# Half of one projection and a quarter of another by Strassen blocks in the prologue of a two-branch attention kernel

## The chip, the cores and the metric

The kernel runs on one core of one Trainium2 chip. The metric is the device time of one execution in microseconds; the runs of a kernel are given by their median. The engines are named as the profile names them: PE (matmuls; PEld is its weight load), DVE, ACT, POOL and SP, whose queue issues most DMAs.

## What is computed

x has 2048 tokens of 1024 features. A linear-attention branch A and a softmax-attention branch B share x, have 32 heads of 32 features each, and are mixed by a gate per token:

```python
g = _sigmoid((x * gate_w).sum(-1, keepdims=True))
# A: phi(t) = where(t > 0, t + 1, exp(t)) + 1e-6
kv  = einsum("bhsd,bhse->bhde", phi(k), v)
z   = einsum("bhsd->bhd", phi(k))
num = einsum("bhqd,bhde->bhqe", phi(q), kv)
den = einsum("bhqd,bhd->bhq", phi(q), z)[..., None] + 1e-6
a   = (num / den) @ A_wo
# B
p = softmax(einsum("bhqd,bhkd->bhqk", q, k) * Dh ** -0.5)
b = einsum("bhqk,bhkd->bhqd", p, v) @ B_wo
return g * a + (1 - g) * b
```

Each branch has its own wqkv (1024 x 3072), so the projections x @ wqkv are most of the dense work.

## The kernel before

**Numbers in two parts.** Every projection operand is split into a high part (rounded to fp32r) and a low part; a product is three matmuls, high x high, high x low, low x high (`three`, L146 to L158). A split is one ACT cast (L302) and one subtraction, on DVE (L297, by `split`) or on POOL (L869, by `split_w`). A full matmul is 128 x 128 weights by 512 columns.

**Prologue.** J counts two halves of the tokens. For each, `v_pass` computes B's v for its first 512 of 1024 columns directly, over eight row pieces k, into all eight PSUM banks, and `v_out` (L369) copies them out and stores them. Beside it DVE forms the sums of x that Strassen's method needs (`sides`, `split_sides`, `last_side`). Then eight quads compute B's q and k by Strassen's method: seven products in place of eight, with `quad_weights` preparing the next quad's weight sums and splits, and `quad` combining the products on DVE and storing q and k. A generator `wo_parts` runs beside the quads on POOL and prepares sums of wo. The weights of v are kept in a ring of tile halves (`RINGW`, `ring_w`), stored (`store_wv`, q `wv<-big`) and reloaded for J = 1. In the last quad, `leave` splits the weights of the first linear chunk on DVE and `load_first` loads q and k of heads 0 and 1 by POOL's DMA queue (L1224, L1237).

**The linear stream.** After the prologue everything is a stream of units, one per chunk of 512 output columns and tile of 128 tokens, 24 matmuls each. The chunks in order: v's second half (1 chunk, 16 units), four kv chunks (256 key and 256 value columns, 64 units), two q chunks, two o chunks. A kv unit applies phi (ACT L918 to L920, DVE L1147), adds the keys for z on POOL (L1150, L1152) and multiplies keys by values in small matmuls (`keys`, L938). Weights of the next chunk are loaded and split while the last unit of a chunk runs: on DVE if the chunk that ends is v, else on POOL (`renew`, `split_w`).

**The heads.** Softmax attention of the 32 heads of B runs in the same time as the units. `maxima` computes the scores of a head once for their maxima (PE L1263, DVE L1268). `heads_` computes them again, transposed, with the maximum subtracted, and ACT takes the exponent (PE L1405, ACT L1408) into one of nine tiles `pr_t`. POOL sums the tiles for the denominator (L1486 the first, L1490 the others; 1536 of 2048 columns, DVE takes the other 512 in L1506; beside q units POOL takes all). Every eight tiles, PE multiplies them by v (L1555). At a head's end POOL issues two accumulating DMAs that fold the sum (L1444, L1445); `finish` multiplies it by ones on PE (L1327), at the next head's first L1555 group, and DVE divides. `rows` transposes the maxima once per head (L1280).

**The planner.** The order of instructions on every engine is written out at build time. The loop at the end keeps a planned clock T for each engine, with costs as constants (0.2275 us a matmul, 0.15 + 0.0022 us per column for a POOL sum), and picks the stream that can start. Linear units are paced against score steps: `rates` is the number of matmul slots per step (64 steps of L1405 per head), computed from `cost`, the slots of all kv, q and o units. Before the heads begin there is a warm-up: `warm` slots of linear units and the maxima of head 0 and the first 12 of head 1, which are spread over it (`behind`). SP's and POOL's queues are in order like the engines.

**The gate.** `gate_step` takes one of 32 pieces of x every GATE_STEP planned microseconds: SP loads it, ACT scales it by the gate weights (L594), POOL adds it up (L600), and PE sums over partitions (L608). Before, this lies in the warm-up, beside v's second half.

Of the kernel before, what the change touches and what calls it, by code (L numbers as in the profile page):

```python
# [19 lines left out]
P = 128  # L20
DH = 32
# [17 lines left out]
WARM = 8  # L39
NE = 3  # L40
AHEAD_X = 3
PIECE_STEP, PIECE_REST = 3.4, 2
GATE_STEP, GATE_FROM = 2.3, 20.0
# [6 lines left out]
def kernel(  # L50
# [271 lines left out]
    for side in PLACES:  # L322
        side["X12"] = side["T4"]
    NQB = 8
    RINGW = [(16, 0), (16, 1), (17, 0), (17, 1), (19, 0), (19, 1), (14, 0), (14, 1), (20, 0), (20, 1), (15, 0),
             (18, 0), (18, 1)]
# [4 lines left out]
    def ring_w(n, p):  # L331

        b, half = RINGW[n % len(RINGW)]
        return big[b][:, (2 * half + p) * C:(2 * half + p + 1) * C]

    def v_ring(J, k):
        return J * (NK + QUADS * NP) + k

    def quad_ring(J, f, s):
        return v_ring(J, NK) + f * NP + s  # L340
# [14 lines left out]
    assert not {b for b, _ in RINGW[:NK]} & set(RAW_BIG)  # L355
# [7 lines left out]
    v_outs = [[P1, C11, H11, *halves(zrep), W2, *halves(zrep)], [P1, C11, W2, H11] * 2]  # L363
    wv_d = [dram.tile([P, 2 * C], F32, name=f"wv{k}") for k in range(NK)]
# [147 lines left out]

    def wo_piece(m, i):
        half, l = int(m[1]) - 1, int(m[2]) - 1
        return b_wo[(2 * i + l) * P:(2 * i + l + 1) * P, half * C:(half + 1) * C]
# [58 lines left out]
    gate_x = [mid[7], mid[8], mid[9], zrep[:, :C]]  # L574

    def gate_step():
# [11 lines left out]
        raw, acc = gate_x[n % len(gate_x)], (mid[6], zrep[:, C:])[j % 2]  # L588
# [45 lines left out]
    def split_wv(raw, k):  # L634
        split(ring_w(k, 0), ring_w(k, 1), raw, nc.vector)
# [35 lines left out]
    def late_side(J):  # L671

        yield
        yield
        last_side(J, (0, 1))
        yield
        last_side(J, (2, 3))

# [5 lines left out]
    def quads(J, first, *others):  # L684

        sides_ = [late_side(J), *others]
        for f in range(QUADS - 1):
# [4 lines left out]
            quad(J, f, beside(quad_weights(raws_q[(f + 1) % 2], J, f + 1), *sides_))  # L692
# [9 lines left out]
    for k in range(NK):  # L702
# [12 lines left out]
        if k == 4:  # L715
            load_quad(raw_a, 0)
        if k >= 5:
            store_wv(((0, 1, 2), (3, 4, 5), (6, 7))[k - 5])
        if k == 6:
            for _ in spill(0, "X12"):  # L720
                pass
    for b in RAW_BIG:
        big[b] = big_tile(b, F32R)
    w_t[2] = big[18]
    quad_w = quad_weights(raw_a, 0, 0)
    for _ in range(3):
        next(quad_w)
    split_sides(raw_x0[3], 0, 3)
    for _ in quad_w:
        pass  # L730
    load_quad(raw_b, 1)
    for t, to in enumerate(v_outs[0]):
        v_out(0, t, bank[t], to)

# [21 lines left out]
    quad(0, QUADS - 1, change())  # L756
    for k in range(NK):
# [5 lines left out]
        elif k == 1:  # L763
            sides(raw_x1[1], 1)
            split_sides(raw_x1[1], 1, 1)
            load_pair(raw_x1[3], 1, 3)
        elif k == 2:
            for kk in (4, 5):
# [3 lines left out]
        elif k == 3:  # L772
# [5 lines left out]
            load_quad(raw_a, 0)  # L778
            for _ in spill(1, "X12"):
                pass  # L780
        elif k == 4:
            split_sides(raw_x1[3], 1, 3)
            load_quad(raw_b, 1)
        elif k == 5:
            quad_w = quad_weights(raw_a, 1, 0)
            next(quad_w)
            next(quad_w)
        elif k == 6:
            for _ in quad_w:
                pass  # L790
# [3 lines left out]
    def load_v1(raws, ks):  # L794
        for raw, k in zip(raws, ks):
            dma(raw, b_wqkv[k * P:(k + 1) * P, 2 * D + C:2 * D + 2 * C])

    def split_v1(raw, k):
        split(wpart(k, 0), wpart(k, 1), raw, nc.vector)

    quads(1, lambda: load_v1(raw_a, range(KH)), spill_rest(1), parts)
    load_v1(raw_b, range(KH, NK))

    def leave():

        split_v1(raw_a[2], 2)
        split_v1(raw_a[3], 3)
        yield
        split_v1(raw_a[0], 0)
        split_v1(raw_a[1], 1)  # L810
        yield
        for k in range(KH, NK):
            split_v1(raw_b[k - KH], k)
# [18 lines left out]
    chunks = [("v", c) for c in range(1, NQC)] + [("kv", c) for c in range(D // HC)]  # L832
# [21 lines left out]
    def load_w(kind, c, k, n):  # L854
        if kind == "v":
            raw = load_cols(b_wqkv, vcols(c), k, n)
        elif kind == "kv":
# [42 lines left out]
    def token(i, t):  # L900
        return (t + NT // 2) % NT if chunks[i][0] == "v" else t
# [162 lines left out]
    def linear():  # L1064
        extra = iter(())
        for n, (i, t) in enumerate(units):
            kind, c = chunks[i]
            follow = chunks[i + 1] if i + 1 < len(chunks) else None
            lag = 2 if kind == "v" else 0
# [879 lines left out]
```

## Time and profile before

| what | value |
|---|---|
| median of 3 runs (lowest, highest) | 2807.05 us (2806.37, 2807.08) |
| span of the profiled execution | 2803.6 us, 3.4 us under the median |
| PE busy, PE weight load busy | 2794.3 us, 2040.4 us |
| DVE busy | 2327.5 us |
| ACT busy | 1640.2 us |
| POOL busy | 2104.4 us |
| granted clock | 1.000 |

A row of a group names line, engine, operation, tile written <- tiles read, shape and count; then busy time and mean nanoseconds of one; then the engine's idle time before these instructions and what ended it. Busy digits are tenths of each of 40 slices. Window rows give the length, then busy microseconds (and instructions) of PE, PEld, DVE, ACT and POOL, the clock, the DMA share and GB/s. The profiled execution is one execution; its span runs from the first to the last instruction, and the timed runs contain a little more around it.

### The profile page before, as it was taken

Reading aid. Unit: us, or ns where it says so; the run is one execution under the profiler, and the core shown is the slowest. Engines: PE = TensorE matmul, PEld = TensorE weight load, DVE = VectorE, ACT = ScalarE, POOL = GpSimd, SP = SyncE. Lnnn points to the kernel's source line nnn. Section 1 sums busy time; section 2 is a strip of 40 time slices with the busy share of each in tenths; the row PEclk is TensorE's granted clock in tenths of the full one; section 3 lists DMA queues with packets and bytes.
Section 4 is the critical chain, followed back from the end, with each engine's and each line's share of the span. In section 5 each row is a group of like instructions: output and inputs, shape, how many; then the busy total and the mean of one; then the engine's idle time right before and its main releaser. Section 6 shows DMA issues by size and latency. Waiting matters only on the chain.

```text
span 2803.6 us, 46986 instructions
## 1 busy us (share of the span) xinstructions
PE 2794.3 (100%) x15880; PEld 2040.4 (73%) x15880; DVE 2327.5 (83%) x3745; ACT 1640.2 (59%) x3095; POOL 2104.4 (75%) x1150
## 2 busy tenths in 40 slices
PE   9999999999999999999999999999999999999999
PEld 8888888776677767777667777776676667666687
DVE  7978956888888888888888888888887888886688
ACT  5334323666676666666666676676666666666522
POOL 0642543799999999999899988889889988888000
PEclk9999999999999999999999999999999999999999
DMA  8997979433444334333433444455575555544774
GB/s 286 314 327 232 319 225 287 153 99 107 104 120 109 99 95 125 99 102 97 135 98 102 107 129 133 148 175 178 176 222 145 147 159 150 144 122 150 253 234 152
DMA packets 403340, 459.52 MB, mean 164 GB/s; under 512 B 106894, under 2 KB 234894, under 8 KB 401308
## 3 DMA queue, kind: packets, MB, share of 16 engines
q1 hardware_dynamic: 381084, 419.03, 48.6%
q0 software_dynamic: 22016, 37.50, 6.3%
q8 instruction: 126, 2.06, 0.3%
q14 instruction: 114, 0.93, 0.1%
HBM read 314.31 MB, written 127.66 MB: 158 GB/s over the span
## 4 chain that ended last, share of the span: by engine, by line
PE 91%; DMA 3%; DVE 1%; issue 1%; SPq 0%; ACT 0%; ACTq 0%; DVEq 0%
PE bank L1405 17%; PE bank L1263 17%; PE bank L1555 16%; PE bank L153 13%; PE bank L158 13%; PE bank L156 13%; PE bank L1327 1%; PE bank L1049 1%; DMA big<-wv 1%; SPq L170 0%; DMA big<-ra 0%; DMA xs<-big 0%; PE bank L938 0%; DMA mid<-in_xT 0%; DMA extra<-in_xT 0%
## 5 line engine op out<-in xcount | busy, mean ns | idle before, releaser
L1490 POOL TENSOR_TENSOR big<-big,big 128x512 f32<-128x512 f32 (+2 forms) x694 | 1642.0, 2370 | 106.9 <-ACT big L1408 63.8
L1268 DVE TENSOR_REDUCE mx<-bank 128x1 f32<-128x512 f32 x2048 | 1314.3, 684 | 301.1 <-PE bank L1263 297.5
L1408 ACT ACTIVATE big<-bank 128x512 f32<-128x512 f32 x2048 | 1180.0, 602 | 427.8 <-PE bank L1405 362.4
L1405 PE MATMUL bank<-big,big 128*128 128x512 f32 x1888 | 741.5, 394 | 0.1
L1263 PE MATMUL bank<-big,big 128*128 128x512 f32 x1888 | 739.0, 391 | 0.0
L153 PE MATMUL bank<-big,big 128*128 128x512 f32 x1576 | 616.0, 391 | 2.8 <-ACT big L302 1.2
L156 PE MATMUL bank<-big,big 128*128 128x512 f32 x1576 | 614.2, 390 | 0.0
L158 PE MATMUL bank<-big,big 128*128 128x512 f32 x1572 | 613.2, 390 | 0.2 <-DMA big<-xs 0.2
L1555 PE MATMUL bank<-big,mid 128*32 128x512 f32 x4096 | 454.2, 593 | 0.0
L1405 PEld LDWEIGHTS bank<-big,big 128*128 128x128 f32 x1888 | 354.0, 188 | 124.7 <-issue 47.4
L1263 PEld LDWEIGHTS bank<-big,big 128*128 128x128 f32 x1888 | 354.5, 188 | 73.7 <-ACT big L1408 1.4
L153 PEld LDWEIGHTS bank<-big,big 128*128 128x128 f32 x1576 | 296.0, 188 | 69.5 <-ACT big L302 2.6
L158 PEld LDWEIGHTS bank<-big,big 128*128 128x128 f32 x1572 | 295.1, 188 | 63.6 <-DVE big L297 1.0
L156 PEld LDWEIGHTS bank<-big,big 128*128 128x128 f32 x1576 | 295.9, 188 | 61.3 <-DVE big L297 0.2
L1555 PEld LDWEIGHTS bank<-big,mid 128*32 128x32 f32 x4096 | 143.6, 110 | 264.3 <-issue 264.0
L1506 DVE TENSOR_TENSOR bank<-bank,big 128x512 f32<-128x512 f32 x364 | 252.2, 693 | 5.5 <-ACT big L1408 3.3
L302 ACT CAST big<-mid 128x512 fp32r<-128x512 f32 (+1 forms) x157 | 92.9, 618 | 122.5 <-DVE mid L1674 66.0
L1486 POOL TENSOR_TENSOR big<-big,big 128x1536 f32<-128x1536 f32 (+1 forms) x31 | 123.4, 3980 | 40.3 <-ACT big L1408 40.1
L153 PE MATMUL bank<-big,xh 128*128 128x512 f32 x376 | 147.0, 391 | 0.6 <-DVE mx L1268 0.6
L158 PE MATMUL bank<-big,xh 128*128 128x512 f32 x376 | 146.9, 391 | 0.3 <-DMA xh<-xs 0.3
L156 PE MATMUL bank<-big,xh 128*128 128x512 f32 x376 | 146.8, 390 | 0.0
L1563 ACT COPY mid<-bank 128x512 f32<-128x512 f32 x32 | 18.8, 587 | 212.8 <-PE bank L1555 205.8
(165 smaller groups left out, 2226.4 us busy)
## 6 DMA issues: line engine op xcount, KB each, us to landing
big<-xs SPq DMA_DIRECT2D x288, 256.0 KB
big<-qk SPq DMA_DIRECT2D x690, 64.0 KB
xh<-xs SPq DMA_DIRECT2D x144, 256.0 KB
qk<-mid SPq DMA_DIRECT2D x128, 256.0 KB
big<-oA SPq DMA_DIRECT2D x84, 256.0 KB
xs<-big SPq DMA_DIRECT2D x64, 256.0 KB
oA<-mid SPq DMA_DIRECT2D x64, 256.0 KB
big<-big POOLq DMA_DIRECT2D x50, 256.0 KB, 5.4
```

The lines of the kernel that those rows point to most:

```text
L153: yield nc.tensor.matmul(ps, sh, mh_, start=(kt == 0), stop=False)
L156: yield nc.tensor.matmul(ps, sh, ml_, start=False, stop=(late and last))
L158: yield nc.tensor.matmul(ps, sl, mh_, start=False, stop=last)
L302: nc.scalar.copy(hi, src)
L1263: nc.tensor.matmul(bank[b], q[:, t % TPC * P:(t % TPC + 1) * P], k[:, j * C:(j + 1) * C], start=True, stop=True)
L1268: nc.vector.tensor_reduce(m[:, t, j:j + 1], bank[b], AX.X, ALU.max)
L1405: nc.tensor.matmul(bank[b], k[:, t * P:(t + 1) * P], q_cols(h, j), start=True, stop=True)
L1408: nc.scalar.activation(pr_t[i][:, j * C:(j + 1) * C], bank[b], AF.Exp, scale=SCALE)
L1486: nc.gpsimd.tensor_add(lacc[:, :qp], pr(0)[:, :qp], pr(1)[:, :qp])
L1490: nc.gpsimd.tensor_add(lacc[:, sl], lacc[:, sl], pr(t)[:, sl])
L1506: nc.vector.tensor_add(lacc[:, qp:] if t == NT - 1 else l_b[:, :n], l_b[:, :n], src)
L1555: nc.tensor.matmul(av_b[j * DH:(j + 1) * DH, :], v[:, t, :], pr(t)[:, j * C:(j + 1) * C], start=(t == 0), stop=(t == NT - 1))
```

## The change

v's second half and the first of the four kv chunks leave the linear stream. After each `v_pass`, a new function `block` computes both for that half of the tokens as one 2 x 2 Strassen product: weight column half 1 is v's second half, column half 2 the 256 key and 256 value columns. The seven products run in the order below. Products that belong to the same output accumulate in PSUM without being copied out first (`onto`). Weights are loaded by `load_side`, summed on DVE (`sums`) and POOL (`sums4`) and split on DVE, one product ahead, between two alternating sets of ring places (`SETS`). Keys and values of the chunk go through phi, the z sums (POOL) and the small key products inside the block, and a partial z per J goes through DRAM (`zs_d`).

The first quad's weights, which were prepared at the end of `v_pass`, are now prepared in the block's last products. The linear stream starts with the second kv chunk, whose weights `leave` splits on DVE. The warm-up is seven units long instead of sixteen. The gate's pieces come every 4.5 planned us instead of 2.3, so that they reach into the first heads, and use three loading tiles instead of four.

```diff
+WARM_UNITS = 7
-GATE_STEP, GATE_FROM = 2.3, 20.0
+GATE_STEP, GATE_FROM = 4.5, 20.0
...
+    BLOCK = [("X11", "W11"), ("X21", "W12"), ("T2", "S2"), ("T1", "S1"), ("T3", "S3"), ("T4", "W22"), ("X22", "S4")]
...
+    def block(J, w11, w12, w21, w22, quad_w, renew):
...
+        steps = {
+            (0, 0): lambda: split_n(1, w12, 0, 1),
+            (0, 1): lambda: split_n(1, w12, 2, 3),
+            (0, 2): lambda: sums(0),
+            (0, 3): lambda: sums(1),
+            (1, 0): lambda: (sums(2), split_n(2, w11, 0, 1)),
...
+            (1, 2): lambda: (split_n(2, w11, 3), sums4(), load_quad(raw_a, 0), last_side(J, (0,))),
...
+            (5, 3): lambda: (early_kv(2, 3), renew(), next(quad_w), z_sums(range(4))),
+            (6, 0): lambda: (later_kv(0, 1), next(quad_w)),
...
+        for n, (name, m) in enumerate(BLOCK):
+            onto = name in ("T2", "T3", "T4", "X22")
+            at = 0 if name in ("X11", "T2", "T3", "T4") else TPC
+            for kt in range(KH):
+                wh, wl = (ring_w(SETS[J][n % 2][kt], p) for p in range(2))
+                for i in range(TPC):
+                    xh_, xl_ = (xpiece(J, name, p, kt)[:, i * P:(i + 1) * P] for p in range(2))
+                    for u, (x_, w_) in enumerate(((xh_, wh), (xh_, wl), (xl_, wh))):
+                        nc.tensor.matmul(bank[at + i], x_, w_, start=(kt == u == 0 and not onto),
+                                         stop=(kt == KH - 1 and u == 2), skip_group_check=onto)
...
+        if k == 3:
+            load_side(raw_a, "W11")
+        elif k == 4:
+            load_side(raw_big[0], "W21")
         if k >= 5:
             store_wv(((0, 1, 2), (3, 4, 5), (6, 7))[k - 5])
         if k == 6:
+            load_side(raw_big[1], "W12")
+            for i in range(2):
+                block_split(0, 0, i, raw_a[i])
             for _ in spill(0, "X12"):
                 pass
-    quad_w = quad_weights(raw_a, 0, 0)
...
+        elif k == 7:
+            load_side(raw_big[2], "W22")
...
     for t, to in enumerate(v_outs[0]):
         v_out(0, t, bank[t], to)
+    split_sides(raw_x0[3], 0, 3)
...
+    block(0, raw_a, raw_big[1], raw_big[0], raw_big[2], quad_weights(raw_a, 0, 0), renew_0)
...
-    chunks = [("v", c) for c in range(1, NQC)] + [("kv", c) for c in range(D // HC)]
+    chunks = [("kv", c) for c in range(1, D // HC)]
...
-                next_w.append((follow, k, mark, nc.vector if kind == "v" else nc.gpsimd))
+                next_w.append((follow, k, mark, nc.gpsimd))
...
-    warm = (NQC - 1) * NT * pace
-    cost = {"kv": NT * (D // HC) * (pace + 1) + 2 * (D // HC), "q": NQC * NT * (pace + 2),
+    warm = WARM_UNITS * pace
+    cost = {"kv": NT * (D // HC - 1) * (pace + 1) + 2 * (D // HC) - warm, "q": NQC * NT * (pace + 2),
             "o": NQC * NT * pace}
...
-            part = (lin_done[0] - 6 * pace) / (warm - 7 * pace) if warm else 1.0
+            part = (lin_done[0] - pace) / (warm - 2 * pace)
```

`pace` is 24, the slots of a unit; `lin_done` counts the slots done. `block` for J = 1 is called in the same way after the second `v_pass`.

241 lines of the change are left out of this document (169 added, 72 removed).

## The prediction

> **What bounds the kernel now.** I read the page first, its busy times and slices:
>
> ```profile
> span 2803.6 us, 46986 instructions
> PE 2794.3 (100%) x15880; PEld 2040.4 (73%) x15880; DVE 2327.5 (83%) x3745; ACT 1640.2 (59%) x3095; POOL 2104.4 (75%) x1150
> POOL 0642543799999999999899988889889988888000
> PEclk9999999999999999999999999999999999999999
> ```
>
> PE has no idle time to speak of and its clock never drops. A busy PE could still be a slow one, so the timeline of PE comes second, in the last projection product before the linear stream:
>
> ```profile
> 398.73 0.39 PE L153 MATMUL bank<-big,big 128*128 128x512 f32 x1
> ...
> 400.09 0.39 PE L153 MATMUL bank<-big,big 128*128 128x512 f32 x1
> ```
>
> Six matmuls start in 1.36 us, one every 0.2267 us. That is the price of a full matmul here; work taken off PE is worth its price as long as nothing else is as late as PE. The POOL digits ask whether that holds: 0 to 7 tenths in the prologue (the first seven slices), 8 and 9 in the heads. So the third view is the heads, in which three things share PE: the maxima of one head, the probabilities of another, and the linear units that fill in. One row transpose (L1280) is issued per head; the first row below has 18 of them, all in heads that run beside kv units. The next two count the matmuls of line 153, one in three of a linear unit's, in the same stretch.
>
> ```profile
> L1280 PE MATMUL bank<-ident,mneg x18: 270/271/272, 557.9 to 1644.2; 128*16 128x128 f32 x18
> L153 PE MATMUL bank<-big,big 128*128 128x512 f32 x312 | 122.0, 391 | 0.0
> L153 PE MATMUL bank<-big,xh 128*128 128x512 f32 x160 | 62.6, 391 | 0.0
> ```
>
> 17 heads take 1086.3 us, so PE needs 63.9 us a head, and (312 + 160) x 3 / 17 = 83.3 of its matmuls belong to linear units.
>
> What does POOL need for a head? It sums the probabilities (L1486, L1490), issues two DMAs that fold the sum (L1444, L1445), and adds the keys for z (L1152). A stretch where POOL is behind and never waits gives its own pace: from the fold of one head at 1420.6 us to the fold three heads later at 1600.0 us.
>
> ```profile
> 1420.60:1480.20 59.60, 59.60 (x404) 41.96 (x403) 51.25 (x89) 38.15 (x75) 57.97 (x30) 1.00 0.36 95
> 1480.20:1540.00 59.80, 59.80 (x388) 41.29 (x387) 51.31 (x88) 38.70 (x77) 57.81 (x29) 1.00 0.40 107
> 1540.00:1600.00 60.00, 60.00 (x405) 42.26 (x404) 51.53 (x89) 39.00 (x75) 58.44 (x30) 1.00 0.38 99
> L1490 POOL TENSOR_TENSOR big<-big,big 128x1536 f32<-128x1536 f32 x30 | 106.2, 3538 | 1.8
> L1490 POOL TENSOR_TENSOR big<-big,big 128x512 f32<-128x512 f32 x36 | 46.0, 1285 | 2.1
> L1486 POOL TENSOR_TENSOR big<-big,big 128x1536 f32<-128x1536 f32 x3 | 12.9, 4293 | 0.0
> L1152 POOL TENSOR_TENSOR mid<-mid,mid 128x256 f32<-128x256 f32 x10 | 8.9, 893 | 0.0
> L1445 POOL DMA_DIRECT2D big<-big x3 | 4.3, 1418 | 0.0
> L1444 POOL DMA_DIRECT2D big<-big x4 | 4.0, 1008 | 1.6 <-POOL big L1490 1.6
> ```
>
> (The windows' columns after the length are PE, PEld, DVE, ACT and POOL.) The groups show 174 us of work and only short hand-over gaps, no wait for another engine. So POOL's own head is 59.8 us, with 3.3 z-adds in it. Once per 16 units, that is every 4.6 heads, eight weight subtractions (L869) of 1.3 us come on top, 2.2 us a head:
>
> ```profile
> L869 POOL TENSOR_TENSOR big<-big,big 128x512 fp32r<-128x512 f32 x27 | 34.7, 1298 | 8.4 <-ACT big L867 6.6 <-PE bank L156 1.5 <-DMA mid<-in_a_wqkv 0.3
> ```
>
> PE is the bound by 63.9 to 62.0: a lead of three per cent, and it exists only because linear units sit in the heads. The change takes units out of exactly there.
>
> How much lateness can POOL afford? What waits for it first is the fold: PE's matmuls on the folded sum (L1327) stand at a fixed place in PE's order, in the next head's first product of probabilities and values.
>
> ```profile
> L1486 POOL TENSOR_TENSOR big<-big,big x31: 3496/4133/4628, 518.1 to 2531.7; 128x1536 f32<-128x1536 f32 x26, 128x2048 f32<-128x2048 f32 x5
> 577.36 1.46 POOL L1445 DMA_DIRECT2D big<-big  x1
> DMA to landing us min/median/max: 6.2/6.2/6.2
> 598.56 0.62 PE L1327 MATMUL bank<-big,ones 64*32 64x256 f32 x9
> ...
> 1420.62 1.42 POOL L1445 DMA_DIRECT2D big<-big  x1
> DMA to landing us min/median/max: 6.8/6.8/6.8
> 1429.21 0.45 PE L1327 MATMUL bank<-big,ones 64*32 64x256 f32 x8
> ```
>
> For the first head the fold lands at 583.6, 15.0 us before PE asks. For the head in which a set of weights was split, it lands at 1427.4, only 1.8 us before. One split set ate the slack; the next heads give it back at 63.9 - 59.8 = 4 us each.
>
> **The change part by part.** *PE work.* v's second half was 16 units of 24 matmuls, and the first kv chunk 16 more: 768. By Strassen it is two blocks of 7 products x 4 row pieces x 4 tiles x 3 = 336: 672. 96 matmuls less, x 0.2267 = -21.8 us. The small key products of those 16 units become two batches with as many matmuls:
>
> ```profile
> L938 PE MATMUL bank<-mid,mid 128*32 128x32 f32 x1024 | 15.7, 199 | 0.0
> ```
>
> 15.7 us for 64 units is 0.25 a unit, 4 us for 16; batching can save at most a part of that, and I take 0. Nothing hides the 21.8 us but what is late next.
>
> *Length of a head.* The planner's rate for kv and o units is (kv cost + o cost - 24) over 1728 steps. Before: (1608 + 768 - 24)/1728 = 1.361 matmul slots a step, 87.1 a head. After, the kv cost is 48 units x 25 + 8 - 7 x 24 = 1040, so (1040 + 768 - 24)/1728 = 1.032, 66.1 a head, 63.2 of them matmuls of units (24 of 25). PE's head becomes 63.9 - 20.1 x 0.2267 - 0.2 (0.84 units at 0.25) = 59.1 us. POOL's becomes 59.8 - 0.7 z-adds x 0.89 = 59.2 us. They are equal: from here on, whatever else POOL has to do in the kv heads (1040/66.1 = 15.7 of them) stands in full on the path once the slack is gone.
>
> *Gate.* Its POOL adds now end before the heads begin:
>
> ```profile
> L600 POOL TENSOR_TENSOR mid<-mid,mid x10: 1272/1290/1295, 428.5 to 483.4; 128x512 f32<-128x512 f32 x10
> L600 POOL TENSOR_TENSOR zrep<-zrep x4: 1286/1290/1463, 457.6 to 507.6; 128x512 f32<-128x512 f32 x4
> L1405 PE MATMUL bank<-big,big x1888: 387/389/504, 508.5 to 2633.0; 128*128 128x512 f32 x189
> ```
>
> They cost nothing there, since POOL was idle. After, the heads begin after 168 unit slots and 76 maxima, 244 x 0.2267 = 55 us, some 60 with the key products; the first sum follows 10 us later (508.5 to 518.1). The gate steps every 4.5 us from 20 us on, its add 8 us behind: by 70 us nine of 32 steps are through, and about 20 of the 28 adds remain, x 1.29 = 25.8 us on POOL in heads 0 and 1. Its 32 loads on SP and 32 scalings on ACT (ACT is at 39 of 60 us above) fit; one accumulating DMA that POOL issues for z is 1.4 us, as L1445, and lies within the ends below. Of POOL's lateness, the first head has 15.0 us of slack, less what PE's shorter head takes: the 80.5 us from the first sum to L1327 become 80.5 x 59.1/63.9 = 74.5. So 25.8 - 15.0 + 6.0 = 16.8 us of waits by the end of head 1.
>
> *Splits.* Before, four sets come in kv heads; after, the first is split by DVE in the prologue, and those for the third and fourth kv chunk and for q remain. Two lie amid kv heads: 2 x 8 x 1.3 = 20.8 us, with no slack left. The q set falls where q units lengthen the heads; 3 us for it. The other 14 heads at 0.1: 1.4 us. POOL in all: 16.8 + 20.8 + 3 + 1.4 = 42. Ends: if PE's head proves 1 us longer than reckoned, or POOL's shorter, 14 us are given back, and if some gate adds come earlier another 6: 22. The other way: 55.
>
> These are waits of 6 to 11 us on PE, and the trace has none like them:
>
> ```profile
> 560.00:1640.00 1080.00, 1079.87 (x6981) 760.67 (x6980) 938.03 (x1588) 718.27 (x1391) 1013.32 (x507) 1.00 0.39 106
> ```
>
> In this stretch of heads PE is idle for 0.13 us and the granted clock is 1.00, so I price a wait at its length. [...]
>
> *Entering the first block.* ACT copies eight banks out before it can cast the weights of the second product; the seventh copy waits for a tile still being stored.
>
> ```profile
> 47.63 1.64 SPq L170 DMA_DIRECT2D v<-mid  x3
> 49.38 1.92 SPq L170 DMA_DIRECT2D v<-zrep  x2
> 53.88 1.22 ACT L369 COPY zrep<-bank 128x512 f32<-128x512 f32 x2 [3.85 <-DMA v<-zrep]
> 24.00:44.00 20.00, 20.00 (x90) 16.57 (x89) 19.73 (x32) 9.85 (x19) 0.00 (x0) 1.00 1.09 362
> ```
>
> Before, the first quad's weights were cast ahead of these copies. After, SP has W21, W12 and W22 queued ahead of the stores in place of one quad load: 2 MB more, at the 362 GB/s of the last row 6 us. The copy comes at 60, then another, four casts and a subtraction (0.5 to 0.6 each: 9.85 us for ACT's 19, 19.73 for DVE's 32 in that row): 63. The first product (48 matmuls, 10.9 us) starts when the pass ends, where the stores begin, 47.8, and ends at 58.7. So 4 us; between 0, if DMAs overlap better, and 9. In the second block the loads are far ahead: 0. Inside the blocks DVE and ACT have per product (10.9 us) four splits and four adds, some 5 us each at these prices: hidden.
>
> *Earlier maxima.* The planner lets the maxima begin after 24 unit slots instead of 144: the first comes about 6 us into the stream instead of 33; the keys for its second quarter come by POOL's queue:
>
> ```profile
> 402.93 2.46 POOL L1237 DMA_DIRECT2D big<-qk  x5
> DMA to landing us min/median/max: 5.0/5.6/5.9
> L1263 PE MATMUL bank<-big,big x1888: 387/389/583, 432.2 to 2572.4; 128*128 128x512 f32 x189
> ```
>
> The stream began near 399.4; the fifth maximum would come at about 407 and its keys land at about 409, those of the third quarter a few us later: 3 us (0 to 6). Behind this wait stand only units, on the same PE.
>
> Sum: -21.8 + 42 + 4 + 3 = +27, with the ends -21.8 + 22 = 0 and -21.8 + 55 + 9 + 6 = +48. Against the profiled span of 2803.6 that is 2831; the median of the runs, 2807.05, lies 3.4 us above the span for what is around it, and I carry this over: 2834. I place the forecast a little lower, at 2830, since the slack of 15 us is the tightest of POOL's deadlines and not all of them.
>
> **Rivals.** (1) *POOL keeps up, and the matmuls saved are seen.* If PE's head stays over POOL's by 2 us or more (units pulled later, more key products, fold landing earlier than asked), 15 heads return 30 us, which with the initial slack covers gate and splits. For it: before, four split sets cost PE nothing. Against it: that took 4 us a head, and 20.1 matmuls are gone. It decides at a POOL head of about 57.5 us. Time: 2807 - 21.8 + 4 + 0 to 4 = 2791, or 2785 to 2797 with the ends of the small terms. (2) *The two cancel.* POOL costs 15 to 25 us: 2802 to 2812. [...] (4) *DVE becomes the bound.* In the 1080 us of heads above it is busy for 938, 55.5 of 63.9 us a head: that is 94% of 59.1. It would add under 5 us to any case.
>
> **How the numbers follow.** Forecast 0.53 (2813 to 2845), rival 1 0.27, rival 2 0.13 (half of it on either side of 2807), rival 3 0.07. About 0.2%, 5.6 us, is what a measurement of this kernel can tell from no change. Faster by more: 0.27; within: 0.13; slower: 0.53 + 0.07 = 0.60. The range of 2788 to 2846 leaves out a third of rival 1, most of rival 3 and little else.
>
> **What would show it.** Right: in the kv heads the fold lands when L1327 asks, PE's L1327 or its weight load shows idle time put down to POOL or the fold's DMA, POOL is over 97% busy from the first head to the q units, and the L1280 period is about 60 to 62 us, longer in heads 0 and 1. The block's second product waits for ACT. Wrong: L1280 every 59 us with a slack of 5 us or more at L1327 in the middle of the kv heads; or POOL idle, waiting for ACT, in those heads; or a PE total that did not fall by some 96 matmuls.

## The result and the profile after

The changed kernel takes 2973.66 us (median of 4 runs, 2970.17 to 2975.44), beside 2806.71 (2804.22 to 2807.08) for the kernel before: a ratio of 1.0592, 95% interval 1.0577 to 1.0607. It is 167 us slower, where the prediction had 23.

In the changed kernel most line numbers have moved: the three matmuls of a unit or product are L154, L157 and L159, maxima L1418 (PE) and L1423 (DVE), scores L1560, exponentials L1563 (ACT), POOL's sums L1641 and L1645, its fold DMAs L1599 and L1600, PE's fold product L1482, row transposes L1435. The gate scales in L750 (ACT), adds in L756 (POOL) and totals in L764; the keys for z are L1307 and L1309 (POOL) behind DVE's L1304; the weights for POOL's subtraction L1032 are cast in L1030. The block's products are L642. The page of the changed kernel:

```profile
span 2973.7 us, 46720 instructions
PE 2853.1 (96%) x15784; PEld 2028.6 (68%) x15784; DVE 2392.2 (80%) x3843; ACT 1627.6 (55%) x3103; POOL 2107.3 (71%) x1149
POOL 0163026347657799999999998998899999999200
PEclk9999999999888899999999999999999999999999
```

The 96 matmuls are gone (15784 for 15880), and POOL's work is what it was (2107 for 2104 us). But PE now has 120 us without work, four slices have a lower clock, and POOL is at 5 to 7 tenths just there, in the first heads. The waits of PE in the prologue and up to the first heads, from the view of waits (engine, tile and line, releaser; us in total, times, longest):

```profile
PE bank L154 <- DMA big<-wv: 14.2, 1, 14.2
PE bank L1418 <- DMA big<-qk: 4.6, 1, 4.6
PE bank L642 <- ACT big L303: 3.2, 1, 3.2
PE bank L642 <- DVE big L298: 0.5, 1, 0.5
```

The second is the wait of the earlier maxima, which the prediction costed at 3 us; the last two are the wait at the entry of the first block, costed at 4. The first is new: a reload of v's weights, at 260 us. The heads come next. One row transpose is issued per head, so the starts of L1435 give their lengths: 59.6 us for head 0, then 86.2, 98.5, 95.7, 87.7 and 65.1, and from head 6 to head 14 about 60.5, except 67.9 for head 9, in which weights are split. Heads 1 to 4 as windows, and below them a stretch behind them for comparison:

```profile
689.00:775.00 86.00, 68.79 (x391) 42.30 (x390) 53.61 (x90) 42.11 (x85) 55.55 (x34) 0.88 0.36 97
775.00:873.00 98.00, 74.70 (x381) 46.30 (x379) 60.66 (x97) 41.90 (x85) 65.63 (x34) 0.86 0.27 70
873.00:969.00 96.00, 70.91 (x383) 43.83 (x382) 55.41 (x93) 41.42 (x84) 67.59 (x36) 0.86 0.27 70
969.00:1057.00 88.00, 73.11 (x380) 45.86 (x381) 58.10 (x97) 41.34 (x84) 63.33 (x30) 0.88 0.26 66
1122.00:1665.00 543.00, 536.05 (x3367) 354.25 (x3366) 483.31 (x815) 355.76 (x692) 526.77 (x257) 0.99 0.37 93
```

The columns behind the length are PE, PEld, DVE, ACT, POOL, clock, DMA share and GB/s. In the 368 us of heads 1 to 4 every engine has idle time. POOL, which was to be the bound, works 252 us, 69%. PE is idle for 80.5 us. It also works 287.5 us for 1535 matmuls (those across a window's edge counted twice), 0.187 each, where the last row has 0.159; the difference, 43 us, goes with the clock of 0.86 to 0.88. So some 124 us are lost here, two thirds to idling and one third to a slower PE. What POOL waits for in these four heads:

```profile
POOL mid L1309 <- ACT big L1563: 23.2, 2, 12.7
POOL mid L1309 <- DVE mid L1304: 22.1, 4, 8.6
POOL zrep L756 <- ACT mid L750: 18.8, 5, 10.2
POOL mid L1307 <- PE bank L1560: 13.4, 1, 13.4
POOL big L1032 <- ACT big L1030: 10.6, 6, 7.6
POOL mid L756 <- ACT mid L750: 9.6, 2, 8.3
```

POOL never waits for the exponentials that its sums need (there is no row of L1645), but nearly always for the inputs of small additions and splits. Yet ACT's exponentials wait 86.6 us in the same stretch for POOL's sums:

```profile
ACT big L1563 <- POOL big L1645: 86.6, 18, 13.1
```

Pairing each sum with its exponentials in the trace, the sums of head 1 start 35 to 57 us after the last exponential that they need. POOL idles with ready work behind the instruction at which it stands. One turn of this, in rows taken from the timelines of three engines (start, us, engine, line; in brackets the idle time before; rows between them are left out):

```profile
739.52 1.27 POOL L756 TENSOR_TENSOR mid<-mid,zrep 128x512 f32<-128x512 f32 x1 [3.80 <-ACT zrep L750]
741.89 2.61 POOL L1645 TENSOR_TENSOR big<-big,big 128x512 f32<-128x512 f32 x2
743.18 1.08 ACT L1563 ACTIVATE big<-bank 128x512 f32<-128x512 f32 x2 [2.51 <-POOL big L1645]
743.83 1.22 PE L1560 MATMUL bank<-big,big 128*128 128x512 f32 x2 [3.19 <-ACT big L1563]
745.47 1.42 POOL L1600 DMA_DIRECT2D big<-big  x1
752.32 1.10 PE L1482 MATMUL bank<-big,ones 64*32 64x256 f32 x14 [2.74 <-DMA big<-big]
753.50 0.36 ACT L1485 COPY bank<-bank 128x256 f32<-128x256 f32 x1 [5.33 <-PE bank L1482]
753.77 0.72 ACT L750 ACTIVATE mid<-mid,omg_sb 128x512 f32<-128x512 f32 x1
754.58 1.28 POOL L756 TENSOR_TENSOR zrep<-zrep,mid 128x512 f32<-128x512 f32 x1 [4.22 <-ACT mid L750]
```

POOL waits 3.8 us for a scaling of the gate. Only when it has done the sums behind does ACT's next exponential run, and only then PE's next score. The fold goes out late, PE waits for it at L1482, ACT's copy waits for PE, the next scaling of the gate stands behind that copy, and POOL, with the next sums of this head behind it, waits 4.2 us for the scaling.

### The profile page after: what moved, and what is told of

Same layout as the page of the kernel before. It is cut to its first block, busy times and chain, and to the rows that moved or that the text cites. A ratio compares the mean times of both kernels' runs of the same rounds, so it can differ in the third digit from the quotient of the medians.

```text
span 2973.7 us, 46720 instructions
## 1 busy us (share of the span) xinstructions
PE 2853.1 (96%) x15784; PEld 2028.6 (68%) x15784; DVE 2392.2 (80%) x3843; ACT 1627.6 (55%) x3103; POOL 2107.3 (71%) x1149
## 4 chain that ended last, share of the span: by engine, by line
PE 72%; DVE 11%; POOL 4%; DMA 3%; ACT 2%; issue 2%; SPq 0%; DVEq 0%; POOLq 0%; ACTq 0%
PE bank L1710 14%; PE bank L1560 14%; PE bank L1418 12%; PE bank L154 9%; PE bank L157 9%; PE bank L159 9%; DVE mx L1423 6%; POOL big L1645 3%; PE bank L642 3%; ACT big L1563 1%; DVE bank L1661 1%; DMA big<-big 1%; DVE bank L1492 1%; DMA big<-wv 1%; PE bank L1482 1%
## 5 line engine op out<-in xcount | busy, mean ns | idle before, releaser
L1645 POOL TENSOR_TENSOR big<-big,big 128x512 f32<-128x512 f32 (+2 forms) x694 | 1640.9, 2368 | 76.2 <-ACT big L1563 32.3
L1423 DVE TENSOR_REDUCE mx<-bank 128x1 f32<-128x512 f32 x2048 | 1288.0, 683 | 308.2 <-PE bank L1418 305.0
L1563 ACT ACTIVATE big<-bank 128x512 f32<-128x512 f32 x2048 | 1153.2, 604 | 487.8 <-PE bank L1560 339.7
L1560 PE MATMUL bank<-big,big 128*128 128x512 f32 x1888 | 742.3, 404 | 51.1 <-ACT big L1563 44.5
L1418 PE MATMUL bank<-big,big 128*128 128x512 f32 x1888 | 738.3, 400 | 20.5 <-ACT big L1563 12.1
L154 PE MATMUL bank<-big,big 128*128 128x512 f32 x1408 | 555.3, 394 | 16.0 <-DMA big<-wv 14.2
L157 PE MATMUL bank<-big,big 128*128 128x512 f32 x1408 | 552.9, 393 | 0.0
L159 PE MATMUL bank<-big,big 128*128 128x512 f32 x1404 | 551.7, 393 | 1.0 <-DVE big L298 1.0
L1560 PEld LDWEIGHTS bank<-big,big 128*128 128x128 f32 x1888 | 357.5, 191 | 192.5 <-ACT big L1563 57.2
L1418 PEld LDWEIGHTS bank<-big,big 128*128 128x128 f32 x1888 | 359.4, 191 | 116.9 <-ACT big L1563 20.4
L1710 PEld LDWEIGHTS bank<-big,mid 128*32 128x32 f32 x4096 | 132.9, 111 | 283.7 <-issue 282.2
L154 PEld LDWEIGHTS bank<-big,big 128*128 128x128 f32 x1408 | 266.9, 190 | 77.3 <-DMA big<-wv 14.7
L159 PEld LDWEIGHTS bank<-big,big 128*128 128x128 f32 x1404 | 265.8, 189 | 59.4 <-DVE big L298 2.5
L157 PEld LDWEIGHTS bank<-big,big 128*128 128x128 f32 x1408 | 266.7, 189 | 55.2 <-DVE big L298 0.2
L303 ACT CAST big<-mid 128x512 fp32r<-128x512 f32 (+1 forms) x169 | 100.3, 618 | 138.7 <-DVE mid L1829 66.0
L298 DVE TENSOR_TENSOR big<-mid,big 128x512 fp32r<-128x512 f32 (+1 forms) x138 | 100.1, 741 | 80.4 <-ACT big L303 80.2
L642 PE MATMUL bank<-big,big 128*128 128x512 f32 x672 | 154.8, 392 | 3.7 <-ACT big L303 3.2
L642 PEld LDWEIGHTS bank<-big,big 128*128 128x128 f32 x672 | 127.3, 190 | 30.9 <-ACT big L303 3.6
L1641 POOL TENSOR_TENSOR big<-big,big 128x1536 f32<-128x1536 f32 (+1 forms) x31 | 132.8, 4284 | 17.2 <-ACT big L1563 17.2
```

What stands on the lines that cost most here:

```text
L154: yield nc.tensor.matmul(ps, sh, mh_, start=(kt == 0), stop=False)
L157: yield nc.tensor.matmul(ps, sh, ml_, start=False, stop=(late and last))
L159: yield nc.tensor.matmul(ps, sl, mh_, start=False, stop=last)
L642: nc.tensor.matmul(bank[at + i], x_, w_, start=(kt == u == 0 and not onto), stop=(kt == KH - 1 and u == 2), skip_group_check=onto)
L1418: nc.tensor.matmul(bank[b], q[:, t % TPC * P:(t % TPC + 1) * P], k[:, j * C:(j + 1) * C], start=True, stop=True)
L1423: nc.vector.tensor_reduce(m[:, t, j:j + 1], bank[b], AX.X, ALU.max)
```

## The experiments

The first four runs go by theory A: the loss is the late reload, and gate additions in the heads that make POOL late, so that engines wait for each other. Its rivals: the leaner heads alone (B), the gate's loads (C). Ratios are to the kernel before on the same chip.

**ring.** In the changed kernel, the reload of place 18a is written ahead of the last product that reads 18a. So that product, one of the seven of a quad, waits for the reload and multiplies by weights of v in place of its own. This is so in every run of the changed kernel without this edit, and it doesn't change the amount of work.

```diff
-    STARTS = [SETS[0][0] + SETS[0][1], spots("19a 19b 17b 18a 18b 14b 16a 16b")]
+    STARTS = [SETS[0][0] + SETS[0][1], spots("19a 19b 17b 14b 18a 18b 16a 16b")]
```

> One line of the prologue's weight ring is put in another order: the reload of the v weights that was written to place 18a ahead of the last product that still reads it goes to 14b, and 18a and 18b are written one step later each. Theory A (PE's 14.63 us wait at 260.3 us is that reload, ordered ahead of the product, and the half clock behind it about 2.7 us more): the wait goes, and the time falls by 14 to 18 us, to 2956 to 2960 us; heads 1 to 5 stay as long as they are. Rival: another transfer is as late at that place, and the time falls by less than 5 us. In the kernel as it was, that product read weights of v that had been reloaded in place of its own.

2957.63 us, ratio 1.0537 (1.0519 to 1.0554): 16.0 us less, as theory A has it. The same stretch in the changed kernel, then in this run:

```profile
260.00:275.00 15.00, 0.76 (x5) 0.30 (x3) 6.01 (x10) 2.37 (x4) 4.04 (x6) 0.70 1.03 357
275.00:285.00 10.00, 10.00 (x35) 8.00 (x36) 3.94 (x6) 1.24 (x2) 0.00 (x0) 0.77 0.37 117
```

```profile
260.00:275.00 15.00, 15.00 (x67) 12.40 (x67) 10.21 (x11) 2.39 (x4) 8.42 (x12) 1.00 1.03 352
275.00:285.00 10.00, 10.00 (x46) 8.29 (x45) 6.50 (x11) 5.11 (x9) 0.00 (x0) 1.00 0.98 336
```

After the wait PE gets 35 matmuls into 10 us in place of 46: 11 x 0.2267 = 2.5 us more than the wait itself.

**noadd.** The gate's POOL additions are left out.

```diff
-            if k:
-                plus()
+            if k == NK - 1:
+                total_later()
...
```

> Leaves out the 28 POOL additions of the gate (the gate is then taken from the last products alone); the loads and ACT's scalings of the gate stay. Theory A (the gate's additions in heads 0 to 2 make POOL late, and from then on POOL and ACT, each in order, wait for each other through heads 1 to 5, which cost about 137 us over 5 x 59.1): these heads fall to 60 to 63 us each, and the time to 2835 to 2865 us. Rival B (the heads with one load of keys and values less are POOL-bound and tip over without the gate): the time falls by the additions' own 28 x 1.29 = 36 us or less, to 2935 to 2970 us. Rival C (the gate's loads in SP's queue hold up the linear part's loads): the time falls by less than 15 us.

2850.51 us, ratio 1.0153 (1.0138 to 1.0168): 123 us less for 36 us of work. Heads 1 to 5 take 61.9, 65.8, 63.3, 61.1 and 60.6 us. B and C fall.

**lateadd.** Each addition is issued 6 planned us behind its scaling, and a load whose tile is still in use is put off.

```diff
...
-                plus()
+                gate_busy.append((T["pe"] + 6.0, n, plus))
```

> Each POOL addition of the gate is issued 6 planned us behind ACT's scaling that feeds it, where it was issued in the same step; a load that finds its buffer still in use is put off. Same work. Theory A: POOL's waits for the scalings (50.6 us before L756's instructions in heads 0 to 3) mostly go, and with them the mutual waiting that follows; 40 to 110 us less, 2865 to 2935 us. Rival B (it is POOL's load alone, wherever the additions stand): within 15 us of 2973.7. Rival C (the loads): within 15 us as well.

2986.08 us, ratio 1.0636 (1.0620 to 1.0652): 12 us more. Between 640 and 1060 us POOL's waits at L756 nearly went, but those at L1309 for L1304 grew from 24.5 to 62.6 us. This is a miss for theory A as I had put it: taking the wait for the scalings away gains nothing, since other waits took its place at once.

**dvegate.** The gate on DVE.

```diff
...
-            nc.scalar.activation(raw if k else acc, raw, AF.Copy, scale=gate_wt[:, k:k + 1])
...
             if k:
-                plus()
...
+                nc.vector.scalar_tensor_tensor(acc, raw, gate_wt[:, k:k + 1], acc, op0=ALU.mult, op1=ALU.add)
+            else:
+                nc.vector.tensor_scalar(acc, raw, gate_wt[:, :1], None, op0=ALU.mult)
...
```

> The gate's scaling on ACT and addition on POOL become one DVE instruction each (32, estimated at 0.6 us from the other 128x512 instructions of DVE), so that no engine waits for another in between. Theory A: as without the additions, and DVE, busy for 49 to 54 of 60 us in a head, takes the 19 us over three heads with 0 to 15 us of new waits: 2840 to 2880 us. Rival B: 2935 us or more. Rival C (the loads, which stay): within 15 us of 2973.7.

2893.02 us, ratio 1.0301 (1.0286 to 1.0316). 81 us less, 13 short of the range of A. Heads 0 to 2 take 72.9, 79.1 and 78.0 us: the DVE instructions take 54 us, not 19. Two of the four groups in the source view of the multiply-add's line, with minimum, median and maximum in ns:

```profile
L751 DVE SCALAR_TENSOR_TENSOR zrep<-mid,omg_sb,zrep x10: 1018/1844/3855, 655.8 to 800.1; 128x512 f32<-128x512 f32 x10
L751 DVE SCALAR_TENSOR_TENSOR mid<-mid,omg_sb,mid x9: 730/737/1048, 617.0 to 743.4; 128x512 f32<-128x512 f32 x9
```

The next four split A: the harm lies in heads without slack and additions too dense (A1), or each addition brings its own wait anywhere (A2).

**bgate.** The kernel before, with the gate in the heads. The first quarter of the gate is added up in a tile (`mid[10]`) that v's last copies still use, so the gate's values there are not the kernel's.

```diff
-GATE_STEP, GATE_FROM = 2.3, 20.0
+GATE_STEP, GATE_FROM = 4.5, 90.0
...
-    gate_x = [mid[7], mid[8], mid[9], zrep[:, :C]]
+    gate_x = [mid[8], mid[9], zrep[:, :C]]
...
-        raw, acc = gate_x[n % len(gate_x)], (mid[6], zrep[:, C:])[j % 2]
+        raw, acc = gate_x[n % len(gate_x)], (mid[10], zrep[:, C:])[j % 2]
...
```

> The kernel before with only the gate moved: its 32 steps start with the first head, 4.5 planned us apart, in the buffers that the changed kernel uses; the work is the same. Theory A1 (the gate's additions do harm because the changed kernel's heads leave POOL no slack: 59.1 us of work in a head of 59.1 us, against 59 in 63.8 before): POOL catches up within the next heads, and the time is 2807 to 2835 us. Rival A2 (an addition that waits for ACT in the heads costs about 4.5 us each in any kernel): 2900 to 2935 us.

2935.09 us, ratio 1.0454 (1.0436 to 1.0471). Heads 1 to 5 of a kernel with 4 us to spare in each take 84.6, 112.3, 94.9, 83.5 and 76.1 us, where the kernel before has 63.5 to 64.5. A1 falls.

**spread.** The changed kernel with steps 24 planned us apart, two loading tiles and one adding tile.

```diff
-GATE_STEP, GATE_FROM = 4.5, 20.0
+GATE_STEP, GATE_FROM = 24.0, 20.0
...
-    gate_x = [mid[8], mid[9], zrep[:, :C]]
+    gate_x = [mid[8], mid[9]]
...
-        raw, acc = gate_x[n % len(gate_x)], (mid[10], zrep[:, C:])[j % 2]
+        raw, acc = gate_x[n % len(gate_x)], mid[10]
...
```

> The changed kernel with the gate's 32 steps 24 planned us apart, over the keys' and values' heads, in place of 4.5; POOL's and ACT's work is the same. Theory A1 (28 additions within three heads put POOL so far behind that its in-order queue and those of ACT and DVE wait for each other; spread out they cost their own 36 us of a POOL-bound stretch): the time without the additions, 2850.5, and 20 to 40 us: 2870 to 2890 us. Rival A2 (each addition costs its own time and a wait for ACT of some 2 to 3 us, wherever it stands): 2940 to 2980 us.

3064.75 us, ratio 1.0915 (1.0899 to 1.0931): 91 us more, beyond even A2. The same work, thinned out, hurts longer: heads 3 to 12 take 72.8 to 98.1 us. That rules out A1; the harm comes with each addition. (The fewer tiles alone can't be the reason: the run spreadq below has the same ones.)

**noz.** POOL's additions for z are left out.

```diff
...
-                        nc.gpsimd.tensor_add(zsum[c % 2], zsum[c % 2], pk)
```

> Leaves out POOL's additions of the linear part's key features (zsum; each chunk's first copy stays, so the normalizers of the linear part are those of the last tokens' share only); the gate stays as in the changed kernel. Theory Z (once POOL is late, these additions, which wait for DVE and ACT, carry the mutual waiting on through heads 1 to 5): heads 1 to 5 fall to 60 to 70 us each, and the time to 2840 to 2895 us. Rival (the gate's additions alone hold POOL up; the others only give back their own 0.7 us in each unit, some 2 us a head): 2935 to 2960 us.

2938.09 us, ratio 1.0468 (1.0452 to 1.0484): 36 us less, inside the rival's range. Heads 1 to 4 still take 80.3 to 89.4 us, so the gate's additions alone hold POOL up. They were 86.2 to 98.5, 25.8 us more in all, and the additions left out there were 6.6 us of work: those for z carry a part of the waiting.

**spreaddve.** The ring's line put right, and the gate on DVE 24 planned us apart (the edits of ring, spread and dvegate).

> The changed kernel with the ring's line put right, and the gate on DVE alone, 24 planned us apart. Theory A1: the 123 us that went without the additions and the 16 us of the ring go together, 2834 us; DVE, at 55 of 60.5 us in a head, has 5 us of slack for two or three gate instructions in each: 2830 to 2860 us. Rival (a DVE instruction that reads two operands from SBUF beside a busy POOL is held up, as in the run with the gate on DVE, where it took 0.73 us with POOL idle and 1.0 to 5.3 us beside a POOL sum): DVE becomes the bound in these heads, 2860 to 2900 us.

2910.32 us, ratio 1.0375 (1.0357 to 1.0392), 10 us past the rival's range. The multiply-adds had a median of 2.56 us, and heads 0 to 12 took 62 to 78 us:

```profile
L751 DVE SCALAR_TENSOR_TENSOR mid<-mid,omg_sb,mid x28: 739/2563/5104, 618.8 to 1449.4; 128x512 f32<-128x512 f32 x28
```

The runs lateadd, bgate and spread missed in the same way, and the planner's code shows what they have in common. A sum of exponentials joins a queue (`add_later`) and is issued when POOL's planned clock is free; an addition of the gate or of z is issued on the spot, ahead of all sums in that queue, though it is the newest work. So the next theory, I, is inversion: POOL, in order, stands at the newest addition, whose input comes from ACT or DVE behind exponentials that need the older sums behind it. Theory S says that load alone does it.

**spreadq.** The run spread with both kinds of additions joining the queue; a load is held back while the last addition from its tile is still in it.

```diff
-                    z_end[c % 2] = use("pool", 0.69, end)
...
+                    z_marks[n] = add_later(-1, z_add)
...
-                plus()
+                gate_marks[n] = add_later(-1, lambda: plus(ready))
...
```

> As the run with the gate's steps 24 planned us apart (3064.8 us), but POOL's additions of the gate and of the key features (zsum) join the end of the queue of waiting softmax sums, where they were issued at once, ahead of sums whose exponentials are long done. Same work. Theory I (inversion: POOL idles at such an addition, whose producer on ACT or DVE stands behind exponentials that wait for the very sums queued behind the addition; 78 us before L756 and 113 us before L1307 and L1309 in that run): these waits go, and what is left is the additions' own time: 2870 to 2905 us. Rival S (it is POOL's load in heads that it bounds: the fold comes late, PE waits for it, and all wait for PE): 3000 to 3080 us.

2860.29 us, ratio 1.0196 (1.0179 to 1.0213): 204 us less for an order of instructions, 10 better than expected. The waits of POOL from 640 to 1600 us in spread, then in this run (L756, L1309, L1304 are now L762, L1322, L1315):

```profile
POOL mid L1309 <- DVE mid L1304: 88.5, 17, 10.9
POOL mid L756 <- ACT mid L750: 78.1, 20, 13.3
```

```profile
POOL mid L1322 <- DVE mid L1315: 7.0, 1, 7.0
POOL big L1040 <- ACT big L1038: 2.3, 5, 0.7
```

The gate's wait is gone altogether. S falls.

**denseq.** The same with steps at least 8 apart.

```diff
-GATE_STEP, GATE_FROM = 24.0, 20.0
+GATE_STEP, GATE_FROM = 8.0, 20.0
```

> As the last one, with the gate's steps at least 8 planned us apart. Theory I: 2870 to 2905 us, as the distance matters little once no addition jumps the queue. Rival S: the load in heads 0 to 4 is higher, 2950 to 3010 us.

2866.89 us, ratio 1.0215 (1.0200 to 1.0231), 3 us below the range of I: 16.4 us over the run without additions (noadd). Density matters little once nothing jumps the queue.

**zq.** The changed kernel with z's additions alone in the queue (the first half of spreadq's edit).

> The changed kernel, its gate as it is, with the additions of the key features alone at the end of POOL's queue of sums. Theory I: the waits before L1307 and L1309 (61 us in heads 1 to 5) go, those before L756 (51 us) stay: 2895 to 2945 us. Rival S: within 15 us of 2973.7.

2929.53 us, ratio 1.0440 (1.0425 to 1.0456), 44 us less. Between 630 and 1600 us the waits at z's additions fell from 65.5 to 7.2 us, and those at the gate's stayed (50.1, then 52.8).

**pegate.** The ring's line put right and the gate on PE, in steps 22 planned us apart.

```diff
-GATE_STEP, GATE_FROM = 4.5, 20.0
+GATE_STEP, GATE_FROM = 22.0, 20.0
...
+            for i in range(TPC):
+                nc.tensor.matmul(bank[b][:, i:i + 1], raw[:, i * P:(i + 1) * P], gate_wt[:, k:k + 1], start=True, stop=True)
...
```

> The changed kernel with the ring's line put right, and the gate on PE: each 22 planned us four products of one column (0.25 us each, L764) straight from the loaded tile, added up in a small DVE instruction; nothing of the gate is left on POOL and ACT. Both theories: 2834 us (2850.5 without the additions, less 16 of the ring) and 32 x 0 to 1.0 us, as PE has up to 1.4 us to spare in heads of 60.5 us that POOL bounds: 2834 to 2866 us. If it is over 2880, a wait for a bank or for the tile holds PE up.

2848.62 us, ratio 1.0151 (1.0135 to 1.0166), in the range.

The last six runs ask whether I holds for the kernel before, and what the rest is.

**bdenseq.** The kernel before, its gate in the heads at least 8 planned us apart from 120 on, both kinds of additions in the queue (the edits of spreadq).

> The kernel before with its gate in the heads, at least 8 planned us apart from the end of v's chunk on, and POOL's additions of the gate and the key features at the end of its queue of sums. Theory I (the order of POOL's queue, not the gate's place, made the run with the gate in the heads 2935 us): 2807 to 2830 us, as POOL has 4 to 5 us to spare in each head of 63.8 us for 36 us of additions. Rival (the heads of that kernel do not bear the gate in any order): 2860 us or more.

2819.69 us, ratio 1.0047 (1.0032 to 1.0062). With its gate in the heads that kernel loses 13 us, not 128. Steps, start and tiles differ from bgate as well, but the run spread showed that wider steps alone don't help.

**pegatezq.** pegate, with z's additions in the queue.

> The run with the gate on PE, with POOL's additions of the key features at the end of its queue of sums. Theory I: the 10 us that POOL waits for them there go, 2836 to 2848 us. Rival: they cost nothing any more, as POOL is not late; 2847 to 2852 us.

2844.58 us, ratio 1.0134 (1.0118 to 1.0149): 4 us less than pegate, which the two intervals don't separate. It is the best version of the change that computes everything, and still slower than the kernel before.

**pegatezq20.** pegatezq again, with the planner's rate of linear matmuls beside the query units lowered, so that the heads with key, value and output units take more of them.

```diff
-RATE_Q = 2.6
+RATE_Q = 2.1
```

> As the last one, with the planner's rate of linear work in the queries' heads at 2.1 in place of 2.6, so that the heads of keys and values and of the output take more of it and the queries' heads are shorter and more. If POOL bounds the heads of keys and values by 1.4 us or more, PE's added work there costs nothing: 3 to 12 us less than the last one. If PE bounds them, or POOL the queries' heads, no gain: within 3 us of it, or above.

2855.70 us, ratio 1.0175 (1.0160 to 1.0190): 11 us more. PE's added work in the kv heads was not free, and POOL is at 97 to 98% in most of the longer row of query heads, which take about 75 us.

**pegnoz.** pegate without z's additions (noz's edit).

> The run with the gate on PE, without POOL's additions of the key features (zsum holds only each chunk's first copy), 2.2 us of POOL's work in each of 15 heads. If POOL bounds these heads (60.5 us against PE's 59.1): 15 to 30 us less, 2818 to 2834 us. If PE bounds them: 2844 us or more.

2847.76 us, ratio 1.0148 (1.0131 to 1.0164): no gain on pegate (1.0151). PE had the gate on it here, so POOL alone is tested better by the last two runs.

**ringnoadd.** ring and noadd together.

> The changed kernel with the ring's line put right and the gate's POOL additions left out. If the two losses lie in different places, as the traces have it, they add up: 2850.5 less 16, 2832 to 2837 us. If one had covered part of the other: 2840 us or more.

2835.52 us, ratio 1.0102 (1.0085 to 1.0119): the two losses add up.

**ringnoaddnoz.** The same, also without z's additions.

> As the last one, and also without POOL's additions of the key features (zsum holds only each chunk's first copy): 2.2 us of POOL's work less in each of 15 heads, and no wait of POOL for DVE there. If POOL bounds the heads of keys and values, they fall from 60.5 to 59.1 us each, where PE bounds them: 15 to 28 us less than the last one, 2806 to 2820 us. If something else bounds them: 2827 us or more.

2834.60 us, ratio 1.0101 (1.0086 to 1.0116). Heads 1 to 14 of ringnoadd, then of this run:

```profile
673.00:1536.00 863.00, 851.86 (x5310) 566.19 (x5309) 769.33 (x1293) 574.30 (x1122) 822.85 (x403) 1.00 0.37 98
```

```profile
673.00:1536.00 863.00, 852.29 (x5313) 566.60 (x5312) 772.89 (x1295) 575.89 (x1123) 802.44 (x369) 1.00 0.37 98
```

The fifth number, POOL's, falls by 20.4 us. By the row transposes these 14 heads take 863.3 and then 862.4 us. In head 8 POOL goes from 97% to 93%, and the head takes 60.1 us in both. POOL does not bound these heads.

## Why the prediction was wrong

The 167 us are 16 of the ring, 123 that went with the gate's additions, and 29 that remain (2835.52 against 2806.46). That the last figure looks like the forecast's +27 is luck: ringnoadd has no gate additions, and without the gate's 16.8 the forecast's other terms come to +10. Most of the rest lies in the heads: against the 59.1 us reckoned for each, heads 1 to 14 of ringnoadd are 36 us too long, where the forecast had 22 for the splits and the other heads.

*PE work, -21.8.* Right in its count, 96 matmuls.

*Entering the block, +4, and the earlier maxima, +3.* Right, within their ends: 3.2 + 0.5 and 4.6 us in the waits.

*The ring.* No term had its 16 us. I counted the loads of the new blocks and never followed which product last reads a place before its reload is issued; the order in `STARTS` was in the diff.

*The gate, 25.8 - 15.0 + 6.0 = 16.8.* This is the step that failed: 16.8 us were reckoned, and 123 went with the additions. The size of the work was about right: 24 of the 28 additions, 31 us, stand in heads 0 to 2, where I had about 20 in heads 0 and 1. What failed is "less the slack": I let POOL's lateness be worked off in its own order, as if a late POOL were a busy POOL. I had written that loads and scalings fit, since ACT was at 39 of 60 us. Occupancy was not the question. The addition stood ahead of sums that ACT needed before it could reach the scaling, and so POOL was late and idle. My own list had it as a sign of being wrong: "POOL idle, waiting for ACT, in those heads". The same additions behind the older sums cost 16.4 us in denseq (with z's additions in the queue as well). That this is close to 16.8 is no confirmation: the 16.8 rest on heads that POOL bounds, and ringnoaddnoz shows that without the gate it doesn't; the additions also stand in other heads there (0 to 6).

*Splits, 20.8.* In ringnoadd the heads with a split set, 3 and 9, take 63.3 and 65.9 us beside 60.7 for heads 4 to 7: 8 us together, less than reckoned. (Head 2 takes 65.8 without a split; what lengthens it is open.)

*Length of a head, PE 59.1 and POOL 59.2, hence equal.* In the changed kernel POOL came out at 97% over heads 6 to 14, as forecast, and their period at 60.5; this seemed to confirm the picture and didn't, as ringnoaddnoz shows. In ringnoadd, PE's waits for the fold, which were to be the price of a late POOL, come to 1.3 us in heads 1 to 14. PE is at 852 of 863 us there, and its weight loads wait for others in small pieces, which before they hardly did. From ringnoadd, PE's wait for the fold and four rows of the weight loads:

```profile
PE bank L1485 <- DMA big<-big: 1.3, 2, 0.9
PEld bank L1421 <- DVE mx L1426: 10.0, 28, 0.6
PEld bank L1563 <- DVE bank L1495: 8.4, 10, 0.8
PEld bank L1563 <- DVE mid L1498: 6.2, 8, 0.9
PEld bank L1421 <- ACT big L1566: 6.1, 26, 0.5
```

And the largest rows of weight loads that wait for DVE in the kernel before, from 560 to 1450 us, its heads 1 to 14:

```profile
PEld bank L938 <- DVE bank L1506: 0.8, 2, 0.4
PEld bank L1327 <- DVE mx L1268: 0.4, 1, 0.4
```

The three rows for DVE from ringnoadd have 24.6 us; the two before have 1.2. DVE is busy for 769 of 863 us. This looks like rival 4, to which I gave under 5 us. But that DVE is the bound there is only argued from the waits: no run took work from DVE, and the waits for ACT grew as well, from 6.9 to 21 us in all rows.

*Rival 3, waits that cost more than their length.* It was given 0.07. No run shows the extra time that it put on each wait, but the waits of the changed kernel did cost more than their length: 2.5 us behind the one of 14.2, at a granted clock of 0.50, and about 43 us in heads 1 to 4, at 0.86 to 0.88.

*Rivals 1 and 2.* Rival 1, with 2791, was not near in any version. Rival 2 was also added up wrong: 15 to 25 us of POOL with the other terms (-21.8, +4, +3) give 2807 to 2817, not 2802 to 2812.

## What to carry over

A place in a hand-written order is not only a time but a position ahead of other work: when work is moved to where an in-order engine has a backlog, ask which ready work will stand behind it, and whether its input needs that work. An engine that is late and yet idle is the mark of it; queue such additions behind the older work before judging whether the engine has room. And a busy share of 97% is no proof that an engine is the bound: take work from the engine and see.

## What the runs showed of the hardware

The clock came as a surprise in its size. Around the one idle stretch of 14.2 us in the changed kernel the granted clock was 0.70 over the window with the wait and 0.77 over the 10 us behind it; it was 0.50 from 265.9 to 279.6 us, that is, from 5 us after the wait began to 4.6 us after it ended. In the run ring, without this wait, it was 1.00 in both windows. In heads 1 to 4 of the changed kernel, with waits of PE of up to 11.9 us, it was 0.86 to 0.88 over 368 us; over heads 1 to 14 of ringnoadd it was 1.00.

DVE's multiply-add with both tensors in SBUF took 0.73 to 3.9 us in dvegate and 0.74 to 5.1 us in spreaddve. (The 5.3 us in the expectation of spreaddve are those of a first piece, which has one tensor.) What the long ones go with is seen in the trace of the changed kernel, in DVE's additions and subtractions of 128x512. With all tensors in SBUF, the 423 that overlap no instruction of POOL took 0.68 to 0.69 us; of the 168 that overlap one, 65 took over 0.8 us, up to 2.45, and the 57 of 1.0 us or more all ended 0.54 to 0.56 us after an instruction of POOL had ended, as if they had waited for it. With a tensor in PSUM (`bank`), the 531 that overlap one took 0.67 to 0.70 us. One case, rows of two timelines (start, us), in which DVE ends at 206.79 and POOL at 206.23:

```profile
204.34 2.45 DVE L298 TENSOR_TENSOR big<-mid,big 128x512 fp32r<-128x512 f32 x1
204.93 1.30 POOL L703 TENSOR_TENSOR zrep<-zrep 128x512 f32<-128x512 f32 x1
```

In dvegate the cost, 54 us for 32 instructions, is what made DVE the wrong place for the gate.
